# Kept outputs in PSUM beside the scores, block queries and keys by group, a quarter of one streamed pair on chip

## The chip, the core and the metric

The kernel runs on one core of a Trainium2 chip. The core has four compute engines: TensorE (PE in the profile, its weight loads PEld), VectorE (DVE), ScalarE (ACT) and GpSimd (POOL). SyncE (SP) issues most of the transfers, ScalarE and GpSimd issue a few; all of them share 16 DMA engines. SBUF is the working memory on chip. PSUM is the memory into which TensorE writes: 8 banks of 2 KB in each of the 128 partitions, all of them taken in the part of the kernel that is changed. The metric is device time in microseconds (us) of one execution. The kernel before takes 2104.58 us in the median of 3 runs (2098.04 to 2108.45).

## What is computed

There are two independent halves on 2048 tokens. The first is a convolution layer (a short shift filter, then a long convolution by Fourier transforms); the change doesn't touch it. The second is attention with a recurrent memory:

```python
for s in range(n_seg):                       # 64 segments of 32 tokens
    h = concatenate([mem, x_s])              # 8 memory rows and 32 tokens: 40 rows
    q, k, v = h @ Wq, h @ Wk, h @ Wv         # 32 heads of 128, model width 1024
    scores = where(mask, q @ k.T * scale, -1e9)
    o = (softmax(scores) @ v) @ Wo
    mem = o[:8]                              # the memory of the next segment
    outs.append(o[8:])
```

The next segment's memory is the output of this one, so the 64 segments follow each other. The weights are 32 MB in bfloat16, more than SBUF holds.

## The kernel before, in words

Up to about 390 us the kernel computes the first half, and beside it all queries, keys and values of the last 8 tokens of every segment, which need no memory: 512 rows at once ("block" rows). Block queries and keys go to DRAM as `QKBd`, block values as `VBd`. In the loop over segments only 8 memory rows and 24 tokens are left, 32 columns of `hT`.

A "pair" is a 128x2048 piece of weights: 1024 columns each of Wq and Wk (`("qk", group, chunk)`), of two value blocks (`("v", half, chunk)`), or of two heads of Wo (`("o", group, pair)`). Most pairs stay in SBUF. Those in `STREAM`, 17 in each segment, are loaded again in every segment into a ring of 5 places (`wring`); two are parked in PSUM and copied into the ring (L750, L751). `place` (L679) issues the load of the next streamed pair on SP's queue. `done` calls it as soon as TensorE has used a streamed pair, so a load waits for the place that this release frees, and the ring never holds more than five pairs.

The order of the work in a segment is written out by hand, and each engine runs its instructions in that order. The 32 heads are four groups of 8, u0 to u3. For each group: `qk_part` (L784) multiplies by the 8 chunks, `qk_out` (L790, ScalarE) casts the result to `qks`, `tr_a` transposes it by four matmuls into the tile `tp` (L811) and copies it out (L820, L821 on ScalarE; L819 on POOL adds the block keys from `qkb`), `scores` makes the scores `S` (L841 to L852) and takes off their maximum on VectorE (L855, L856), `softmax` runs on ScalarE and VectorE (L864 to L873), `blocks` copies the probabilities into place (L883), and `pv` (L890) multiplies by the values of the segment and the block values `VB`. `pv` has two results in one PSUM tile: ScalarE copies the outputs of the 32 rows (L894, `OT`), VectorE copies the "kept" outputs of the 8 block rows to `OL` (L896). When all groups are done POOL stores `OL` to DRAM (L898, `OLd`); after the loop all kept outputs are multiplied by Wo together. `wo` (L905) multiplies `OT` by Wo, `Y_sb` is the segment's output (L1013), four stores on POOL write it (L1017), and `fill_mem` (L924, L925) transposes it into `hT`, from which the next segment starts. `h_rows` (L916, L917) has put the next tokens into `hT` before.

The work of different groups is interleaved. Around the change the order is: `pv(u0)`, `blocks(u1)`, two chunks of u3, `tr_a(u2)`, four chunks of u3, `scores(u2)`, `softmax(u2)`, and one group later the same with `pv(u1)`, `tr_a(u3)`, `scores(u3)`. On VectorE the copy of kept outputs in `pv(u0)` stands behind the whole of `softmax(u1)`.

In PSUM four banks park weights, three hold accumulators (`ps_a`), and one (`ps_ts`) serves in turn the transposes `tp`, the scores `S`, the transposed tokens and the transposed memory. `OL` is a bfloat16 tile in SBUF. `load_b` (L825) loads the block queries and keys of all four groups of the next segment in one transfer on SP's queue, behind the scores of u3. `load_vb` (L835) loads `VB` on POOL's queue at the end of a segment, behind the stores of `Y_sb`.

Of the kernel before, what the change touches and what calls it, by code (L numbers as in the profile page):

```python
# [9 lines left out]
BF = mybir.dt.bfloat16  # L10
# [11 lines left out]
def fused_kernel(ctx: ExitStack, tc, q, k, v, shift_k, ssm_k, ssm_D, outa, x, mem0, Wq, Wk, Wv, Wo, outb, n_seg):  # L22
# [18 lines left out]
    PARKED = {("qk", 0, 4): ("v", 0, 2), ("v", 0, 3): ("qk", 1, 6)}  # L41

# [631 lines left out]
    def place():  # L674

        if todo:
            key = todo.pop(0)
            t = ring.tile([128, 2, 1024], BF, tag="wring", name="wring")
            nc.sync.dma_start(t[:], Wst[key])  # L679
            placed.setdefault(key, []).append(t[:])  # L680
# [64 lines left out]
    ps_ts = pp.enter_context(tc.tile_pool(name="b_ps_ts", bufs=1, space=PSUM))  # L745

# [19 lines left out]
    VB = act.tile([128, 256], BF, name="VB")  # L766
# [3 lines left out]
    OL = act.tile([128, 32, 8], BF, name="OL")  # L770
# [37 lines left out]
    def transposes(src):  # L808
        tp = ps_ts.tile([128, 512], BF, tag="ts", name="tp")
        for j in range(4):  # L810
            nc.tensor.transpose(tp[:, j * 128:(j + 1) * 128], src[:, j * 128:(j + 1) * 128], ident[:])  # L811
        return tp

    def tr_a(u):
        tp = transposes(u.qks)
        tv = tp[:].rearrange("e (j t c r) -> e t c j r", j=4, t=2, c=2)
        QK = acte.tile([128, 8, 72], BF, tag="qks", name="QK")
        u.QT, u.KT = QK[:, :, 0:32], QK[:, :, 32:72]
        nc.gpsimd.tensor_copy(u.KT[:, :, 32:40], u.qkb.rearrange("e (h t r) -> e t h r", h=8, t=2)[:, 1])  # L819
        nc.scalar.copy(u.QT.rearrange("e (c j) r -> e c j r", c=2), tv[:, 0])  # L820
        nc.scalar.copy(u.KT[:, :, 0:32].rearrange("e (c j) r -> e c j r", c=2), tv[:, 1])  # L821

    def load_b(s):
        qkb = acte.tile([128, 4, 128], BF, tag="qkb", name="qkb")
        nc.sync.dma_start(qkb[:], QKBd[:, :, s * 128:(s + 1) * 128].rearrange("g e x -> e g x"))  # L825
        return qkb

    def new_u(g):
        u = G()
        u.g = g  # L830
        u.qkb = qkb[:, g, :]
        return u

    def load_vb(s):
        nc.gpsimd.dma_start(VB[:], VBd[:, :, s].rearrange("c g r x -> (c g) r x"))  # L835

    def scores(u):
        S = ps_ts.tile([128, 4, 40], F32, tag="ts", name="S")
        qb = u.qkb.rearrange("e (h t r) -> e h t r", h=8, t=2)
# [45 lines left out]
    def pv(u, s):  # L885
        ot = ps_a.tile([128, 512], F32, tag="a", name="otacc")
        for i in range(2):
            o = ot[:, 160 * i:160 * i + 160]
            for kb, w in enumerate((u.v[:, u.g % 2, :], VB[:])):
                nc.tensor.matmul(o, lhsT=w[:, i * 128:(i + 1) * 128], rhs=PB[:, 2 * kb + i].rearrange("p c q -> p (c q)"),  # L890
                                 start=(kb == 0), stop=(kb == 1))
# [4 lines left out]
        nc.vector.tensor_copy(to[:, 8 * u.g:8 * u.g + 8, :].rearrange("e (c i) r -> e i c r", i=2), ov[:, :, :, 32:40])  # L896
# [15 lines left out]
    def h_rows(H_, hT_, r0):  # L912

        tp = ps_ts.tile([128, 1024], BF, tag="ts", name="x_tp")
# [6 lines left out]
    def fill_mem(hT_, Ysrc):  # L921
        tp = ps_ts.tile([128, 512], BF, tag="ts", name="mt_tp")
# [9 lines left out]
    load_vb(0)  # L932
    qkb = load_b(0)
# [3 lines left out]
    for s in range(n_seg):  # L937
# [11 lines left out]
        qk_part(u0, range(5, 8))  # L949
        qk_out(u0)  # L950
        v_part(0, range(0, 4))
        tr_a(u0)
        unpark()
# [5 lines left out]
        qk_part(u1, range(4, 8))  # L959
        qk_out(u1)  # L960
# [15 lines left out]
        qk_part(u2, range(4, 8))  # L976
        qk_out(u2)
        pv(u0, s)
# [7 lines left out]
        qk_part(u3, range(6, 8))  # L986
        qk_out(u3)
        v_part(1, range(0, 1))
        pv(u1, s)
# [5 lines left out]
        if not last:  # L995
            H = load_h(s + 1)
            qkb = load_b(s + 1)
        softmax(u3, S)
        v_part(1, range(5, 8))
        u2.v = u3.v = v_out()  # L1000
        Y = ps_a.tile([128, 512], F32, tag="a", name="yacc")
        wo(u0, Y)
        pv(u2, s)
# [3 lines left out]
        pv(u3, s)  # L1007
        if not last:
            hT = new_hT()
            h_rows(H, hT, 8)  # L1010
        wo(u3, Y)
# [6 lines left out]
        if not last:  # L1018
            load_vb(s + 1)

# [87 lines left out]
```

## Time and profile before

| what | value |
|---|---|
| three runs | 2098.04, 2104.58, 2108.45 us |
| profiled execution: its time, its span | 2100.65, 2098.9 us |
| the loop over segments | from about 395 to 2022 us |
| after it: the kept outputs by Wo | to 2095 us |
| busy in the span: PE, DVE, ACT, POOL | 81%, 53%, 43%, 20% |
| granted TensorE clock, mean | 0.981 |
| moved by DMA | 728.64 MB, mean 347 GB/s |
| DMA share and rate from 400 to 2010 us | 0.99, 366 GB/s |

The page's second part cuts the span into 40 slices; a digit is the busy share of a slice in tenths. Its sixth part lists the DMA issues with size and time from issue to landing. The chain of waits follows the work that ended last back to what released it; a DMA in it lasts from issue to landing. The timeline lists instructions with their start, their duration, their tile and, in brackets, how long the engine was idle before and what ended that. Matmul ends in it are modelled.

### The profile page before, as it was taken

The page shows a single profiled execution, that of the slowest core. Times are in us where ns is not written, and L with a number is a line of the kernel's source. Part 1 is how long each engine was busy: PE and PEld are TensorE (multiplying, and loading weights), DVE is VectorE, ACT ScalarE, POOL GpSimd, SP SyncE. Part 2 cuts the span into 40 slices and gives each one's busy share as a digit, 9 for nine tenths or more (in the row PEclk, how much of TensorE's full clock was granted, in tenths as well). Part 3 has the DMA queues.
Part 4 walks back from the last instruction along what each step waited for, and adds up shares of the span by engine and source line. Part 5 has one row for each costly group of instructions (what it writes and reads, how often), then busy time and mean ns, then how long its engine had stood idle before and what let it go on. Part 6 is the DMA issues. An engine that isn't in the chain of part 4 may idle for free. (4 is left out here: it accounts for less than half of the span.)

```text
span 2098.9 us, 73980 instructions
## 1 busy us (share of the span) xinstructions
PE 1707.5 (81%) x30484; PEld 893.0 (43%) x30514; DVE 1122.1 (53%) x3368; ACT 910.0 (43%) x2278; POOL 417.6 (20%) x1023
## 2 busy tenths in 40 slices
PE   5888987777878888888888888888888878888779
PEld 3332233344444444444444444444444444444449
DVE  8985833355555555555555555555555555555441
ACT  5556741244444444444444444444444444444430
POOL 3003730111111221111111111111112211111110
PEclk9999999999999999999999999999999999999999
DMA  7799989899999999999999999999999999999980
GB/s 272 260 338 331 351 300 378 313 365 361 367 353 367 373 370 367 366 362 370 379 363 368 359 378 365 365 374 363 374 355 369 366 362 365 369 377 370 344 335 22
DMA packets 266384, 728.64 MB, mean 347 GB/s; under 512 B 65007, under 2 KB 77183, under 8 KB 265277
## 3 DMA queue, kind: packets, MB, share of 16 engines
q1 hardware_dynamic: 239534, 686.72, 88.7%
q0 software_dynamic: 15520, 22.06, 3.3%
q10 hardware_dynamic: 10992, 15.14, 2.1%
q8 instruction: 239, 3.92, 0.7%
q14 instruction: 99, 0.81, 0.1%
HBM read 673.52 MB, written 56.56 MB: 348 GB/s over the span
## 5 line engine op out<-in xcount | busy, mean ns | idle before, releaser
L784 PE MATMUL qkacc<-Wqk,hT 128*32 128x512 bf16 x4096 | 335.5, 380 | 0.0
L784 PEld LDWEIGHTS <-hT 128*32 128x32 bf16 x8192 | 185.8, 96 | 238.0 <-issue 82.3
L905 PEld LDWEIGHTS <-OT 128*32 128x32 bf16 x8192 | 210.3, 96 | 109.3 <-issue 61.3
L784 PE MATMUL qkacc<-wring,hT 128*32 128x512 bf16 x2048 | 205.7, 390 | 24.7 <-DMA wring<-Wstqk 17.8
L751 DVE COPY wring<-park 128x1024 bf16<-128x1024 bf16 x128 | 88.5, 692 | 244.0 <-PE vacc L798 112.9
L864 ACT ACTIVATE P<-S 128x128 bf16<-128x128 f32 x256 | 71.1, 278 | 329.1 <-DVE S L856 257.9
L798 PE MATMUL vacc<-Wv,hT 128*32 128x512 bf16 x2560 | 209.3, 381 | 0.0
L798 PE MATMUL vacc<-wring,hT 128*32 128x512 bf16 x1536 | 154.6, 389 | 62.1 <-DMA wring<-in_B_Wv_dram 60.3
L750 ACT COPY wring<-park 128x1024 bf16<-128x1024 bf16 x128 | 130.7, 1021 | 150.9 <-PE qkacc L784 132.7
L798 PEld LDWEIGHTS <-hT 128*32 128x32 bf16 x4096 | 112.5, 96 | 181.7 <-issue 105.7
L784 PE MATMUL qkacc<-Wearly,hT 128*32 128x512 bf16 x2048 | 165.6, 401 | 24.4 <-DVE hT L925 17.9
L883 DVE COPY PB<-P 32x160 bf16<-32x160 bf16 x896 | 173.1, 193 | 10.6
L868 DVE TENSOR_REDUCE sm<-P 128x4 f32<-128x256 bf16 x256 | 107.5, 420 | 131.0 <-ACT P L865 131.0
L820 ACT COPY QK<-tp 128x256 bf16<-128x256 bf16 x256 | 95.4, 373 | 181.7 <-PE tp L811 181.7
L819 POOL COPY QK<-qkb 128x64 bf16<-128x64 bf16 x256 | 60.8, 237 | 566.3 <-PE tp L811 398.2
L905 PE MATMUL yacc<-wring,OT 128*32 128x256 bf16 x2520 | 126.5, 274 | 38.1 <-DMA wring<-Wsto 36.6
L894 ACT CAST OT<-otacc 128x256 bf16<-128x256 f32 x256 | 98.9, 386 | 127.6 <-PE otacc L890 127.6
L790 ACT CAST qks<-qkacc 128x512 bf16<-128x512 f32 x256 | 151.1, 590 | 2.2 <-PE qkacc L784 1.6
L811 PE MATMUL tp<-ident,qks 128*128 128x128 bf16 x1024 | 101.9, 222 | 57.2 <-ACT qks L790 52.7
L1017 POOL DMA_DIRECT2D out_dram<-Y_sb x256 | 128.6, 509 | 92.1 <-ACT Y_sb L1013 89.8
L890 PE MATMUL otacc<-PB,vsb 128*128 128x160 bf16 x512 | 97.8, 238 | 35.9 <-ACT vsb L805 35.9
L855 DVE TENSOR_REDUCE mx<-S 128x4 f32<-128x160 f32 x256 | 83.1, 325 | 74.5 <-PE S L852 68.4
(219 smaller groups left out, 2973.8 us busy)
## 6 DMA issues: line engine op xcount, KB each, us to landing
wring<-Wstqk SPq DMA_DIRECT2D x448, 512.0 KB, 6.1
wring<-in_B_Wv_dram SPq DMA_DIRECT2D x320, 512.0 KB, 6.6
wring<-Wsto SPq DMA_DIRECT2D x315, 512.0 KB, 6.3
SK<-s_sb SPq DMA_DIRECT2D x8, 1024.0 KB, 5.7
SU<-s_sb SPq DMA_DIRECT2D x8, 1024.0 KB, 6.7
QKBd<-stq ACTq DMA_DIRECT2D x4, 2048.0 KB, 8.2
Kg<-SK SPq DMA_DIRECT2D x16, 512.0 KB, 7.7
Ug<-SU SPq DMA_DIRECT2D x16, 512.0 KB, 8.0
```

Source lines behind the costliest of these rows:

```text
L750: nc.scalar.copy(t[:, 0, :], park[key][0][:])
L784: nc.tensor.matmul(u.qk[p0:p0 + 32, :], lhsT=hT[:, kc, :], rhs=w[:, t, c2 * 512:(c2 + 1) * 512], start=(kc == 0), stop=(kc == 7), tile_pos ...
L790: nc.scalar.copy(u.qks[:], u.qk[:])
L798: nc.tensor.matmul(vacc[0][32 * c:32 * c + 32, :].rearrange("p (n x) -> p n x", n=2), lhsT=hT[:, kc, :], rhs=w[:, :, c * 256:(c + 1) * 256 ...
L811: nc.tensor.transpose(tp[:, j * 128:(j + 1) * 128], src[:, j * 128:(j + 1) * 128], ident[:])
L820: nc.scalar.copy(u.QT.rearrange("e (c j) r -> e c j r", c=2), tv[:, 0])
L868: nc.vector.tensor_reduce(out=sm[:], in_=Pv.rearrange("p b x k -> p x b k"), op=ALU.add, axis=AX.XY)
L883: (nc.vector if by[c] == "D" else nc.gpsimd).tensor_copy(to, src)
L890: nc.tensor.matmul(o, lhsT=w[:, i * 128:(i + 1) * 128], rhs=PB[:, 2 * kb + i].rearrange("p c q -> p (c q)"), start=(kb == 0), stop=(kb == 1))
L894: nc.scalar.copy(u.OT[:].rearrange("e (c i) q -> e i c q", i=2), ov[:, :, :, 0:32])
L905: nc.tensor.matmul(Y[32 * dq:32 * dq + 32, 0:256], lhsT=u.OT[:, hh, 0:32], rhs=w[:, hh % 2, dq * 256:(dq + 1) * 256], start=(u.g == 0 and ...
L1017: nc.gpsimd.dma_start(outb[32 * s:32 * s + 24, dq * 256:(dq + 1) * 256], Y_sb[32 * dq + 8:32 * dq + 32, :])
```

## The change

There are four edits, all in the loop over segments.

1. Of the streamed pair `("qk", 1, 3)` the last 512 of 2048 columns stay on chip in a tile `Wquarter`, loaded once. In every segment `place` loads the other 1536 columns into the ring, and the matmul of these columns reads `Wquarter`.
2. The bank `ps_ts` holds one tile, `TS`. Its first 512 bfloat16 columns serve the transposes and the scores as before. Its other half, as 256 float32 columns, is `OL`: VectorE copies the kept outputs of each group from one PSUM tile to the other. At the end of a segment (`store_kept`) VectorE copies all of `OL` to a bfloat16 tile `OLst` in SBUF, and POOL stores that one. For the last group the copy stands behind `h_rows`.
3. `VB` and `OLst` share one buffer, and `load_vb` is issued after `tr_a(u0)` of the segment that uses it, not at the end of the segment before.
4. Block queries and keys are loaded group by group, 32 KB each, into two buffers in turn. The loads of groups 2 and 3 are issued behind the chunks of u1 and u2 in the same segment, those of groups 0 and 1 of the next segment behind the chunks of u3 and of the second half of the values.

```diff
+    QUARTER = ("qk", 1, 3)
...
-            nc.sync.dma_start(t[:], Wst[key])
+            if key == QUARTER:
+                nc.sync.dma_start(t[:].rearrange("p n d -> p (n d)")[:, 0:1536],
+                                  Wst[key].rearrange("p n d -> p (n d)")[:, 0:1536])
+            else:
+                nc.sync.dma_start(t[:], Wst[key])
...
+    TS = ps_ts.tile([128, 1024], BF, name="ts")
+    OL = TS[:, 512:1024].bitcast(F32).rearrange("e (h r) -> e h r", h=32)
+    Wquarter = act.tile([128, 512], BF, name="Wquarter")
+    nc.sync.dma_start(Wquarter[:], half_src(QUARTER, 1)[:, 512:1024])
...
-    VB = act.tile([128, 256], BF, name="VB")
-    OL = act.tile([128, 32, 8], BF, name="OL")
...
-                    nc.tensor.matmul(u.qk[p0:p0 + 32, :], lhsT=hT[:, kc, :], rhs=w[:, t, c2 * 512:(c2 + 1) * 512],
+                    own = ("qk", u.g, kc) == QUARTER and t == 1 and c2 == 1
+                    nc.tensor.matmul(u.qk[p0:p0 + 32, :], lhsT=hT[:, kc, :],
+                                     rhs=Wquarter[:] if own else w[:, t, c2 * 512:(c2 + 1) * 512],
...
     def transposes(src):
-        tp = ps_ts.tile([128, 512], BF, tag="ts", name="tp")
+        tp = TS[:, 0:512]
...
+    def load_b(s, g):
+        qkbs.append(acte.tile([128, 128], BF, tag="qkb", name="qkb", bufs=2))
+        nc.sync.dma_start(qkbs[-1][:], QKBd[g, :, s * 128:(s + 1) * 128])
...
     def load_vb(s):
+        VB = act.tile([128, 256], BF, tag="VB", name="VB")
         nc.gpsimd.dma_start(VB[:], VBd[:, :, s].rearrange("c g r x -> (c g) r x"))
+        return VB
...
-        S = ps_ts.tile([128, 4, 40], F32, tag="ts", name="S")
+        S = TS[:, 0:320].bitcast(F32).rearrange("p (a k) -> p a k", a=4)
...
-        to = OL[:] if s + 1 < n_seg else OLs[:, s]
-        nc.vector.tensor_copy(to[:, 8 * u.g:8 * u.g + 8, :].rearrange("e (c i) r -> e i c r", i=2), ov[:, :, :, 32:40])
-        if u.g == 3 and s + 1 < n_seg:
-            nc.gpsimd.dma_start(OLd[:, s], OL[:].rearrange("e h r -> e (h r)"))
+        to = OL if s + 1 < n_seg else OLs[:, s]
+
+        def keep():
+            nc.vector.tensor_copy(to[:, 8 * u.g:8 * u.g + 8, :].rearrange("e (c i) r -> e i c r", i=2), ov[:, :, :, 32:40])
+
+        if u.g < 3:
+            keep()
+        return keep
+
+    def store_kept(s):
+        OLst = act.tile([128, 256], BF, tag="VB", name="OLst")
+        nc.vector.tensor_copy(OLst[:], OL.rearrange("e h r -> e (h r)"))
+        nc.gpsimd.dma_start(OLd[:, s], OLst[:])
...
         tr_a(u0)
+        VB = load_vb(s)
...
         qk_part(u1, range(4, 8))
+        u1.qkb = qkbs.pop(0)
+        load_b(s, 2)
         qk_out(u1)
...
-        pv(u3, s)
+        keep = pv(u3, s, VB)
         if not last:
             hT = new_hT()
             h_rows(H, hT, 8)
+        keep()
+        if not last:
+            store_kept(s)
         wo(u3, Y)
...
-        if not last:
-            load_vb(s + 1)
```

More of the change, by code (lines that the diff above doesn't have):

```diff
@@ L818, in tr_a @@
         u.QT, u.KT = QK[:, :, 0:32], QK[:, :, 32:72]
-        nc.gpsimd.tensor_copy(u.KT[:, :, 32:40], u.qkb.rearrange("e (h t r) -> e t h r", h=8, t=2)[:, 1])
+        nc.gpsimd.tensor_copy(u.KT[:, :, 32:40], u.qkb[:].rearrange("e (h t r) -> e t h r", h=8, t=2)[:, 1])
         nc.scalar.copy(u.QT.rearrange("e (c j) r -> e c j r", c=2), tv[:, 0])
         nc.scalar.copy(u.KT[:, :, 0:32].rearrange("e (c j) r -> e c j r", c=2), tv[:, 1])
[L823 to L826, printed above, removed]
+    qkbs = []
+    def load_b(s, g):
+        qkbs.append(acte.tile([128, 128], BF, tag="qkb", name="qkb", bufs=2))
+        nc.sync.dma_start(qkbs[-1][:], QKBd[g, :, s * 128:(s + 1) * 128])
     def new_u(g):
@@ L830, in new_u @@
         u.g = g
-        u.qkb = qkb[:, g, :]
         return u
     def load_vb(s):
+        VB = act.tile([128, 256], BF, tag="VB", name="VB")
         nc.gpsimd.dma_start(VB[:], VBd[:, :, s].rearrange("c g r x -> (c g) r x"))
+        return VB
     def scores(u):
-        S = ps_ts.tile([128, 4, 40], F32, tag="ts", name="S")
-        qb = u.qkb.rearrange("e (h t r) -> e h t r", h=8, t=2)
+        S = TS[:, 0:320].bitcast(F32).rearrange("p (a k) -> p a k", a=4)
+        qb = u.qkb[:].rearrange("e (h t r) -> e h t r", h=8, t=2)
         for c in range(4):
@@ L883, in blocks, with pv @@
                 (nc.vector if by[c] == "D" else nc.gpsimd).tensor_copy(to, src)
-    def pv(u, s):
+    def pv(u, s, VB):
         ot = ps_a.tile([128, 512], F32, tag="a", name="otacc")
@@ L912, in h_rows @@
     def h_rows(H_, hT_, r0):
-        tp = ps_ts.tile([128, 1024], BF, tag="ts", name="x_tp")
+        tp = TS[:, 0:512]
         for half in range(2):
@@ L921, in fill_mem @@
     def fill_mem(hT_, Ysrc):
-        tp = ps_ts.tile([128, 512], BF, tag="ts", name="mt_tp")
+        tp = TS[:, 0:512]
         for half in range(2):
@@ L930, in new_hT @@
         return acte.tile([128, 8, 32], BF, tag="hT", name="hT")
-    load_vb(0)
-    qkb = load_b(0)
+    load_b(0, 0)
+    load_b(0, 1)
     home_o(late_o[7], [homes[i][:] for i in (2, 3)])
@@ L949, in fused_kernel @@
         qk_part(u0, range(5, 8))
+        u0.qkb = qkbs.pop(0)
         qk_out(u0)
@@ L976, in fused_kernel @@
         qk_part(u2, range(4, 8))
+        u2.qkb = qkbs.pop(0)
+        load_b(s, 3)
         qk_out(u2)
-        pv(u0, s)
+        pv(u0, s, VB)
         blocks(u1, "DDDD")
@@ L986, in fused_kernel @@
         qk_part(u3, range(6, 8))
+        u3.qkb = qkbs.pop(0)
+        if not last:
+            load_b(s + 1, 0)
         qk_out(u3)
         v_part(1, range(0, 1))
-        pv(u1, s)
+        pv(u1, s, VB)
         blocks(u2, "DDDD")
@@ L996, in fused_kernel @@
             H = load_h(s + 1)
-            qkb = load_b(s + 1)
         softmax(u3, S)
         v_part(1, range(5, 8))
+        if not last:
+            load_b(s + 1, 1)
         u2.v = u3.v = v_out()
@@ L1002, in fused_kernel @@
         wo(u0, Y)
-        pv(u2, s)
+        pv(u2, s, VB)
         blocks(u3, "DDAA")
@@ L1010, in fused_kernel @@
             h_rows(H, hT, 8)
+        keep()
+        if not last:
+            store_kept(s)
         wo(u3, Y)
```

## The prediction

> **What bounds the kernel now.** I read the page first: the slices of the span, then the DMA issues. The memory's loop runs from about 400 to 2020 us, and in it the DMA engines are busy in nine tenths or more of every slice, at 360 to 378 GB/s, while no compute engine reaches nine tenths.
>
> ```profile
> PE   5888987777878888888888888888888878888779
> DMA  7799989899999999999999999999999999999980
> ...
> wring<-Wstqk SPq DMA_DIRECT2D x448, 512.0 KB, 6.1
> wring<-in_B_Wv_dram SPq DMA_DIRECT2D x320, 512.0 KB, 6.6
> wring<-Wsto SPq DMA_DIRECT2D x315, 512.0 KB, 6.3
> ...
> qkb<-QKBd SPq DMA_DIRECT2D x64, 128.0 KB, 5.1
> ...
> VB<-VBd POOLq DMA_DIRECT2D x64, 64.0 KB, 5.1
> ...
> OLd<-OL POOLq DMA_DIRECT2D x63, 64.0 KB, 5.5
> ```
>
> The last column is issue to landing. A streamed pair is 524,288 B; in the first microsecond of a segment, where the moved rate averages 393 GB/s over 29 segments read in windows of 1 us, that is 1.33 us. Landing 6.1 to 6.6 us after issue means that a pair has some four pairs before it. So the stream is nearly always behind, and DMA time is worth something. How much, the chain of waits tells: it alternates between stretches like these two.
>
> ```profile
> 1736.39 6.77 DMA wring<-in_B_Wv_dram
> 1743.20 0.42 PE vacc L798 x4
> 1743.64 6.77 DMA wring<-Wsto
> 1750.45 0.43 PE yacc L905 x8
> ...
> 1789.48 0.43 DVE sm L868
> 1790.14 0.44 DVE P L870
> 1793.18 0.43 DVE sm L868
> 1793.84 0.44 DVE P L870
> 1794.30 0.45 DVE P L873
> 1796.79 0.49 ACT vsb L805
> 1797.32 0.45 PE otacc L890 x4
> ```
>
> The first is a ring place waiting for its load, round after round. The second, from 1789 to 1797, has no DMA in it: softmax of the second, third and fourth group. Two limits thus lie close together. I therefore read the timeline of the 62 segments between 410 and 2010 us at the same rows (hT ready is the end of L925's copy; "max" the start of L855's reduction of a group; groups 0 to 3; pv the matmuls of L890). Stage, mean, tenth percentile in us: hT ready to max of group 1: 10.06, 9.43. Max 1 to max 2: 3.75, 3.70. Max 2 to max 3: 3.71, 3.70. Max 3 to pv 2: 1.71, 1.69. Pv 2 to pv 3: 2.74, 2.24. Pv 3 to the next hT: 3.60, 3.07. Sums: 25.56, the mean period, and 23.83. The middle (max 1 to pv 2) hardly varies: it is a latency chain through VectorE, and the stream costs nothing there. The other three stages hold the 1.7 us lost to late pairs. I call 23.83 the floor and 25.56 the most that the stream can need, since the DMA share of the loop is 0.99.
>
> **The change part by part.** *The quarter.* In each segment the load of that pair shrinks from 4 KB to 3 KB in each partition. Bounds: nothing, if a shorter packet takes as long; 0.36 us, by the loop's mean of 366 GB/s. I take 0.33 us (a quarter of 1.33), as pairs move at the rate of bytes. The stream's need falls to 25.23. The one resident load costs 0.33 us once.
>
> *Kept outputs beside the scores.* Here the middle chain matters. The rows of one group in it:
>
> ```profile
> 1201.60 0.33 DVE L855 TENSOR_REDUCE mx<-S 128x4 f32<-128x160 f32 x1
> ...
> 1203.35 0.40 PE L811 MATMUL tp<-ident,qks 128*128 128x128 bf16 x4 [0.26 <-ACT qks L790]
> ...
> 1204.11 0.38 ACT L821 COPY QK<-tp 128x256 bf16<-128x256 bf16 x1
> ...
> 1204.35 0.18 DVE L896 CAST OL<-otacc 128x64 bf16<-128x64 f32 x1
> ...
> 1204.68 0.21 PE L852 MATMUL S<-QK,qkb 128*8 128x40 bf16 x8
> ```
>
> The transposes of group 2 (1203.35) start as soon as ScalarE has cast its queries; the kept outputs of group 0 are copied (1204.35) a microsecond later, at the end of softmax 1. Neither waits for the other: one writes a PSUM bank, the other SBUF. In the changed kernel both write the tile TS. I looked at the waits in the built program: the first transposing matmul of group 2 now waits for VectorE's copy of group 0's kept outputs, and that of group 3 for group 1's copy. Both have nothing to do with each other's data. Over 62 segments that copy ends 1.15 us (group 2) and 1.17 us (group 3) after the transposes now start. The new path is a ring: max 1 to the copy's end 2.94 (means of both groups), to the transposes 0.05 (as from L790's cast), to the end of the scores 1.56, to the next max 0.09, so 4.64 in place of 3.75 and 3.71. The middle grows by 0.89 + 0.93 = 1.8 us per segment. The bounds, by the spread of the rows (0.67 to 1.19 of lateness): 1.2 and 1.9. The scores of group 2 now have 0.4 us before VectorE is free for them (mean 13.45 against 13.81), which is in the sum. Queued behind the waiting matmul on TensorE are the rest of group 3's queries and keys, its streamed pairs' releases, the scores and everything after.
>
> The Trainium skill, page "PSUM — Partial Sum Buffer", section "PSUM bank collisions raise a hardware error", tells kernel authors to guard PSUM by bank and 32-partition quadrant and not by address, since a second engine in the same bank collides even at other columns. By the addresses (columns 0 to 511 and 512 to 1023) the change would add no wait and the sum would be 25.23 per segment, 2080 us; by this rule the waits are needed, and the sum is the one below. The built program is on the rule's side; no run here shows a collision.
>
> *Two more VectorE steps.* The copy of the last group moves behind the copy into hT, and a new 128x256 copy out of PSUM follows. ScalarE's cast of the same 128x256 from PSUM takes 0.39 us; bounds 0.33 (a 128x160 on VectorE) and 0.69 (the 128x1024 parking copy). In the timeline VectorE has 1.7 us idle before L925, which the transposes of Y_sb end. They now also wait for this copy, which would end 0.7 us or more ahead of them. Nothing.
>
> *OL's store and VB.* The store issues some 0.4 us later and lands after 5.5 us, about 4 us into the segment. VB's load is now behind group 0's key copy on POOL (mean 5.0 us) and waits for that landing, because both use one buffer: issue about 5.3, landing 5.1 later, 10.4. Its first reader, pv 0, runs at 10.7 on the mean, so late loads will stall some segments. But pv 0's result is needed only by VectorE's copy at max 1 + 2.8; a stall of up to about 1 us ends inside the new wait of TensorE. Behind VB's load on POOL stands the clearing of P, which waits for Y_sb's stores anyway (4 us or more after their issue). Taken as nothing; at most 0.3 us a segment.
>
> *Block queries and keys by group.* Four loads of 32 KB replace one of 128 KB, with the same 512 packets of 256 B. Around the present load the rate falls to 332, 334 and 349 from 393 GB/s, 0.42 us in all. Bounds: a little below nothing (the packets spread out), and +1.3 if each of four costs as much as the one. I take nothing: cost by packets. SP issues three more at 0.37 us, ahead of pair loads; a pair that lands 6.3 us after issue doesn't notice 0.4. Each load waits for the scores two groups back, which SP's queue has passed by then, and is needed some 6 us later against 5.1 of landing.
>
> *Sum.* The floor becomes 23.83 + 1.8 = 25.63, the need of the stream 25.23. The floor is now the greater. What stays of the 1.7 us lost to late pairs? In the longer middle the stream, four pairs behind, goes on, so it gains up to 1.8 us and 0.33 more; against that the ring has five places and cannot run ahead by more. Bounds of the rest: 0 and 1.4 (nothing gained but the quarter). I take 0.35, nearer to nothing because of the depth of the queue. Period 25.98, +0.42; by 63 segments +26 us. The profiled execution took 2100.65 us around its span of 2098.9; 2100.65 + 26 = 2127. The median of the three runs shown is 4 us above that execution, within their spread (2098 to 2108), so I keep 2127.
>
> **The rivals.** *A: the stream stays the limit and hides the wait.* For it: a DMA share of 0.99, landings of 6.3 us. Then 25.23 a segment, -21 us, 2080. The point that decides is whether the wait adds less than 1.4 us (25.23 - 23.83). Against: both rows give 0.9, and the lowest values of all six stages still add up to 23.6, which with 1.8 is above 25.23. Chance 0.06.
>
> *B: all that was lost to late pairs is paid back.* The floor alone, 25.63: +4 us, 2105. For it: the queue's depth. Against: DMA would still be wanted 98% of the time, and the tenth percentile of all stages at once is seldom met. With a little rest it reaches 2115. Chance 0.20.
>
> *C: the forecast,* a rest of 0.15 to 0.85: 2115 to 2158, likeliest 2127. Chance 0.56.
>
> *D: the ring has run as far ahead as it can before the new waits,* so that they are added nearly whole: 25.56 + 1.8 - 0.33 = 27.03, +93, 2194. For it: TensorE's waits for pairs stand just outside the middle, five places are 6.7 us of stream, and SP's queue waits for releases (334.7 us in all for those of the queries and keys). Against: pairs there too land only 6 us after issue. From 2158 to 2194, chance 0.18.
>
> The quarter does what it says: the built program loads 1536 of 2048 columns and one matmul in four reads the resident tile.
>
> **How the numbers follow.** No change means within 0.5%, 10.5 us, about what a measurement of this kernel tells. A is faster: 0.06. B ends at the bound of 2115: 0.20. C and D lie above it: 0.74. The range leaves out A and D's upper half, 0.15 together: 2096 to 2172.
>
> **What would show it.** Max 1 to max 2 and max 2 to max 3 at 4.6 us in place of 3.7; TensorE's transposes idle on VectorE's copy into ts, near 1.2 us and more, 126 times; fewer waits of vacc and yacc for wring; a DMA share below 0.99; pv 0 waiting for VB now and then. Wrong would be: the middle at 3.7 (the wait isn't there), or the middle at 4.6 and the period at 25.2 (A), or pairs landing after 7 us or more because of the small loads.

## The result, and the profile after

The changed kernel takes 2228.1 us in the median (2215.76 to 2231.78), the kernel before 2107.27 us (2098.04 to 2110.39) beside it. The ratio is 1.056, 95% interval [1.053, 1.059]: slower by some 118 us. The forecast was 2127, with a range of 2096 to 2172. The side was right, the size far off.

The profiled execution after took 2215.76 us, the least of its six, around a span of 2213.9. First its page: two rows of the slices, then DMA issues (size, median us from issue to landing).

```profile
PE   5798977777777777777777777777777777777759
...
DMA  7789999999999999999999999999999999999960
...
wring<-Wstqk SPq DMA_DIRECT2D x384, 512.0 KB, 5.6
wring<-in_B_Wv_dram SPq DMA_DIRECT2D x320, 512.0 KB, 6.5
wring<-Wsto SPq DMA_DIRECT2D x315, 512.0 KB, 5.5
wring<-Wstqk SPq DMA_DIRECT2D x64, 384.0 KB, 6.7
```

The DMA row still shows nines in nearly all of the loop, and TensorE's row has fallen from sevens and eights to sevens. But pairs of Wo now land 5.5 us after issue instead of 6.3, which fits fewer transfers ahead of them. The next to last slice of the DMA row reads 6 where it read 8. The granted clock is a little lower, 0.965 against 0.981, but TensorE's busy time is the same, 1708.3 and 1707.5 us, so the clock doesn't account for the loss.

Now the step that the prediction spoke of, from the timeline after (start, us, engine and line, tiles, idle time before and what ended it). It goes from one group's reduction of the scores' maximum to the next.

```profile
1201.22 0.33 DVE L867 TENSOR_REDUCE mx<-ts 128x4 f32<-128x160 f32 x1
...
1202.76 0.59 ACT L800 CAST qks<-qkacc 128x512 bf16<-128x512 f32 x1 [0.40 <-PE qkacc L793]
...
1204.02 0.23 DVE L910 COPY ts<-otacc 128x64 f32<-128x64 f32 x1
...
1204.31 0.38 PE L821 MATMUL ts<-ident,qks 128*128 128x128 bf16 x4
...
1205.98 0.33 DVE L867 TENSOR_REDUCE mx<-ts 128x4 f32<-128x160 f32 x1 [1.01 <-ACT QK L831]
...
1208.66 0.20 DVE L910 COPY ts<-otacc 128x64 f32<-128x64 f32 x1
...
1208.91 0.38 PE L821 MATMUL ts<-ident,qks 128*128 128x128 bf16 x4 [1.71 <-DVE ts L910]
...
1210.52 0.33 DVE L867 TENSOR_REDUCE mx<-ts 128x4 f32<-128x160 f32 x1 [0.94 <-ACT QK L831]
```

ScalarE has cast the queries at 1203.35, but the transposes (L821) start at 1204.31, right behind VectorE's copy of kept outputs (L910), which ends at 1204.25. The two steps take 4.76 and 4.54 us, where before it was 3.7. The table of waits after (engine, tile and line; what it waited for; us in total, times, longest) has the same:

```profile
PE ts L821 <- DVE ts L910: 174.4, 124, 2.1
...
POOL QK L829 <- DMA qkb<-QKBd: 123.7, 27, 19.5
```

The second row is new too, and its longest wait is 19.5 us. That one stands in the last segment. The chain of waits after ends with these lines; columns are start, us and what it was.

```profile
2107.78 5.77 DMA wring<-in_B_Wv_dram
2113.55 2.64 issue
2120.42 7.41 DMA wring<-in_B_Wv_dram
2127.91 16.68 DMA qkb<-QKBd
2148.99 2.05 PE yacc L926 x51
2153.46 55.69 PE pl L1062 x928
```

A load of 32 KB is on the path for 16.68 us. The timeline of SP's queue and POOL shows why:

```profile
2121.61 0.43 SPq L996 DMA_DIRECT2D Wv<-Wsto  x1
2122.08 2.97 SPq L996 DMA_DIRECT2D Wqk<-Wsto  x4
...
2125.22 0.94 SPq L999 DMA_DIRECT2D Wearly<-OLd  x2
...
2127.91 0.32 SPq L837 DMA_DIRECT2D qkb<-QKBd  x1
...
2144.74 0.24 POOL L829 COPY QK<-qkb 128x64 bf16<-128x64 bf16 x1 [19.50 <-DMA qkb<-QKBd]
```

In the last segment the loads for the final product (five pairs of Wo, then 4 MB of kept outputs, L996 and L999) are issued ahead of the block keys of group 3, which the segment itself still needs.

Where the time went, by the same stages as in the prediction. Means over the 62 segments, us; "last" is from the last hT to the first weight load of the final product.

| | hT to max 1 | max 1 to 2 | max 2 to 3 | max 3 to pv 2 | pv 2 to 3 | pv 3 to hT | period | last |
|---|---|---|---|---|---|---|---|---|
| before | 10.06 | 3.75 | 3.71 | 1.71 | 2.74 | 3.60 | 25.56 | 22.5 |
| after | 10.42 | 4.69 | 4.68 | 1.89 | 2.28 | 3.21 | 27.17 | 41.4 |

62 times 1.61 is 99.8 us, the last segment adds 18.9, and the parts before the loop and after it together give back some 4: 115, the difference of the two spans. What gives back is mainly a wait of 4.1 us of the final product's first matmul for the kept outputs (`PE pl L1031 <- DMA Wearly<-OLd`), which the kernel before has and the changed kernel, later by then, has not; so the hole costs some 15 us on balance. The middle adds 1.91 per segment, as forecast. What was to be paid back elsewhere is 0.30 on balance instead of 1.4. And the last segment was not in the sum at all.

### The profile page after: what moved, and what is told of

Read it like the earlier page. It is cut to its first block, busy times and chain, and to the rows that moved or that the text cites. A ratio compares the mean times of both kernels' runs of the same rounds, so it can differ in the third digit from the quotient of the medians.

```text
span 2213.9 us, 74498 instructions
## 1 busy us (share of the span) xinstructions
PE 1708.3 (77%) x30484; PEld 908.9 (41%) x30514; DVE 1155.8 (52%) x3431; ACT 915.9 (41%) x2278; POOL 411.3 (19%) x1023
## 4 chain that ended last, share of the span: by engine, by line
DMA 34%; PE 33%; DVE 18%; ACT 7%; issue 5%; SPq 1%; POOL 0%; ACTq 0%; DVEq 0%; POOLq 0%
DMA wring<-in_B_Wv_dram 17%; PE qkacc L793 7%; PE yacc L926 7%; DMA wring<-Wstqk 5%; PE vacc L808 4%; DVE P L885 3%; DVE P L882 3%; DVE sm L880 3%; DMA qkb<-QKBd 3%; PE ts L821 3%; PE pl L1062 3%; PE otacc L902 2%; DMA out_dram<-Y_sb 2%; DVE mx L867 2%; DVE ts L868 2%
## 5 line engine op out<-in xcount | busy, mean ns | idle before, releaser
L793 PEld LDWEIGHTS <-hT 128*32 128x32 bf16 x8192 | 179.3, 96 | 235.9 <-issue 82.0
L821 PE MATMUL ts<-ident,qks 128*128 128x128 bf16 x1024 | 100.9, 221 | 183.7 <-DVE ts L910 174.4
L926 PEld LDWEIGHTS <-OT 128*32 128x32 bf16 x8192 | 218.6, 100 | 56.1 <-ACT OT L906 17.4
L830 ACT COPY QK<-ts 128x256 bf16<-128x256 bf16 x256 | 95.4, 373 | 331.3 <-PE ts L821 214.0
L808 PE MATMUL vacc<-Wv,hT 128*32 128x512 bf16 x2560 | 222.9, 406 | 0.0
L808 PE MATMUL vacc<-wring,hT 128*32 128x512 bf16 x1536 | 157.5, 396 | 76.4 <-DMA wring<-in_B_Wv_dram 75.7
L876 ACT ACTIVATE P<-ts 128x128 bf16<-128x128 f32 x256 | 71.1, 278 | 320.2 <-DVE ts L868 275.7
L867 DVE TENSOR_REDUCE mx<-ts 128x4 f32<-128x160 f32 x256 | 83.2, 325 | 226.7 <-ACT QK L831 114.6
L808 PEld LDWEIGHTS <-hT 128*32 128x32 bf16 x4096 | 104.9, 97 | 207.1 <-issue 86.7
L821 PEld LDWEIGHTS <-qks 128*128 128x128 bf16 x1024 | 67.9, 97 | 266.9 <-issue 146.0
L793 PE MATMUL qkacc<-Wearly,hT 128*32 128x512 bf16 x2048 | 160.0, 389 | 21.8 <-DVE hT L946 17.9
```

Of the source, the lines that this page charges most:

```text
L808: nc.tensor.matmul(vacc[0][32 * c:32 * c + 32, :].rearrange("p (n x) -> p n x", n=2), lhsT=hT[:, kc, :], rhs=w[:, :, c * 256:(c + 1) * 256 ...
L867: nc.vector.tensor_reduce(out=mx[:], in_=S[:], op=ALU.max, axis=AX.X)
L926: nc.tensor.matmul(Y[32 * dq:32 * dq + 32, 0:256], lhsT=u.OT[:, hh, 0:32], rhs=w[:, hh % 2, dq * 256:(dq + 1) * 256], start=(u.g == 0 and ...
```

## The experiments

Unless another kernel is named, every ratio is to the kernel before, run beside it; the interval is 95%. Periods and stages are read as above from one profiled execution of each kernel. Executions of one kernel differ by up to 25 us, that is 0.4 us per segment, so a difference of 0.1 or 0.2 between two periods shows nothing by itself.

**The quarter alone.** The kernel before, with three quarters of the pair loaded.

```diff
+            if key == ("qk", 1, 3):
+                nc.sync.dma_start(t[...][:, 0:1536], Wst[key][...][:, 0:1536])
+            else:
                 nc.sync.dma_start(t[:], Wst[key])
```

> The kernel before with the quarter alone: the pair (qk, 1, 3) is loaded in 1536 of 2048 columns, and the matmul of the other 512 columns reads 512 columns of another resident pair, so part of the second group's keys is computed from other weights; everything else is as before. If the stream's time is what the loop waits for, a quarter pair of 1.33 us gives 0.33 us in each of 64 segments, 21 us less than before (2086), and not less than 10 us. If a shorter packet takes as long, or the latency chain of softmax is the limit, no change.

Measured: 2099.9 us, ratio 0.996 [0.994, 0.998], -8 us or 0.13 per segment. The bytes at the loop's rate would be 0.33.

**Half of that pair not loaded.**

> The kernel before with half of the pair (qk, 1, 3) not loaded in any segment; the matmuls of that half read another resident chunk, so that part of the computation is changed. The same with a quarter gave -8 us, 0.13 us per segment, where a quarter of a pair at the rate of bytes would be 0.33 to 0.36. Theory 'lateness comes from the ring's depth, so that fewer bytes give less than their time': half a pair gives -12 to -25 us (0.2 to 0.4 per segment). Rival 'bytes count in full, and the quarter's run was off': -40 to -46 us (0.65 to 0.72 per segment).

Measured: 2096.3 us, ratio 0.997 [0.994, 0.999], -7 us: no more than for the quarter, and less than the theory's 12 too. Bytes that are taken out here are worth a fraction of their time, and not in proportion.

**The bank alone.** The kernel before with edit 2, `OLst` in a buffer of its own; loads as before.

```diff
+    TS = ps_ts.tile([128, 1024], BF, name="ts")
+    OL = TS[:, 512:1024].bitcast(F32).rearrange("e (h r) -> e h r", h=32)
...
-        tp = ps_ts.tile([128, 512], BF, tag="ts", name="tp")
+        tp = TS[:, 0:512]
```

> The kernel before with the second edit alone: kept outputs as float32 in the bank of the scores, copied to SBUF and stored at the end of a segment. Block queries and keys, VB and the pairs are loaded as before. Theory W (the two new waits of the transposes lengthen the chain by 1.8 us a segment, and the stream pays almost nothing back): the middle stages at 4.6 us, the period at 27.0 us or more, 85 to 110 us more than before (2190 to 2215). Rival G (the waits are mostly hidden, and the small loads of queries and keys cost the rest): the middle at 4.6, but a period of 25.7 to 26.2 us, 10 to 40 us more than before.

Measured: 2212.4 us, ratio 1.048 [1.044, 1.052]; period 27.32, the middle at 4.60 and 4.60, last segment 23.4. In its table of waits:

```profile
PE ts L812 <- DVE ts L899: 193.3, 126, 1.7
...
PE vacc L799 <- DMA wring<-in_B_Wv_dram: 66.7, 109, 2.2
...
PE qkacc L785 <- DMA wring<-Wstqk: 37.2, 62, 1.6
...
PE yacc L915 <- DMA wring<-Wsto: 12.1, 23, 1.3
```

and in that of the kernel before:

```profile
PE vacc L798 <- DMA wring<-in_B_Wv_dram: 60.3, 116, 2.1
...
PE yacc L905 <- DMA wring<-Wsto: 36.6, 76, 1.3
...
PE qkacc L784 <- DMA wring<-Wstqk: 17.8, 34, 1.2
```

The wait on VectorE stands there without any other edit, 126 times. The wait of the Wo products for late pairs has fallen to 12.1 us (36.6 before), but that of the value products has grown from 60.3 to 66.7 and that of the queries and keys from 17.8 to 37.2. In all TensorE waits 116.0 us for pairs, where it waited 114.7: the waits have moved, and none of them is saved. This one edit costs 101 to 105 us.

**The loads by group alone.** The kernel before with edit 4.

```diff
+        u1.qkb = qkbs.pop(0)
+        load_b(s, 2)
         qk_out(u1)
...
-            qkb = load_b(s + 1)
```

> The kernel before with the fourth edit alone: block queries and keys loaded group by group into two buffers. In the last segment the load of the last group stands behind 6.5 MB of final loads on SP's queue, which should cost about 15 us once, as in the changed kernel. Theory W: the period of the other segments stays at 25.5 to 25.7 us, in all 10 to 25 us more than before. Rival G: the period rises by 0.7 us or more, and in all 60 to 100 us more than before.

Measured: 2163.2 us, ratio 1.026 [1.022, 1.030]; period 26.51, last segment 40.6. The edit costed at nothing costs 54 to 56 us. The profiled execution, whose stages these are, took 2173.34 us, some 10 more than the other three: it is 73 us above that of the kernel before, 0.95 in each of 62 segments and some 15 in the last one. In the median execution the part per segment is nearer to 0.7. This lies between theory W and rival G. Its timeline, in two groups of one segment:

```profile
1203.84 0.42 SPq L827 DMA_DIRECT2D qkb<-QKBd  x1
...
1207.14 0.49 SPq L827 DMA_DIRECT2D qkb<-QKBd  x1
...
1210.56 0.24 POOL L819 COPY QK<-qkb 128x64 bf16<-128x64 bf16 x1 [3.40 <-DMA qkb<-QKBd]
...
1210.85 0.23 PE L847 MATMUL S<-QK 128*32 128x40 bf16 x8 [0.78 <-POOL QK L819]
```

POOL waits for block keys, and TensorE's scores wait for POOL: 41 segments of 62 in group 2, 61 of 62 in group 3. The landing takes 5.7 us in the median, which the prediction had; but the loads of groups 2 and 3 go out at 7.96 and 11.55 us of the segment, and POOL wants them at 12.4 and 16.1, by the times of its key copies in the kernel before. That leaves 4.5 us.

**The last segment mended, in the changed kernel.** Group 3's load goes ahead of the final loads in the last segment only.

```diff
         if last:
+            load_b(s, 3)
             spare = ...
...
-        load_b(s, 3)
+        if not last:
+            load_b(s, 3)
```

> The changed kernel with one load moved: in the last segment the block queries and keys of the last group are loaded ahead of the final loads, not behind them. If the hole of 17 us in the last segment comes from that order alone, 14 to 16 us less than the changed kernel (about 2213). If the final loads hold up that segment anyway (something else waits for them), less than 5 us.

Measured: 2207.6 us, ratio 1.046 [1.042, 1.049], 20 us under the changed kernel; last segment 24.8 in place of 41.4, period 27.25 (27.17 unmended). The hole is what it looked like. Some 3 of the 16.6 come back at once, as the final product again waits for its kept outputs; 14 to 16 us were expected, and the larger difference of the two medians lies within what executions differ by.

**The waits taken away, in the changed kernel.** VectorE copies the kept outputs of groups 0 and 1 right behind the sum of the softmax, ahead of its other three steps; ScalarE copies `OT` after that.

```diff
         nc.vector.tensor_reduce(out=sm[:], ...)
+        return P, Pv, sm
+
+    def softmax2(u, P, Pv, sm):
         nc.vector.reciprocal(sm[:], sm[:])
...
         pv(u0, s, VB)
+        softmax2(u1, *sums)
```

> The changed kernel with one step of VectorE's order moved: the kept outputs of groups 0 and 1 are copied right behind the sum of the next group's softmax (1.7 us after its maximum), no longer behind its transpose (2.9 us after); ScalarE's copy of the 32 rows follows it. The copies still go to the bank of the scores. Theory W (the wait of the transposes is what the bank costs): the copy ends about when the transposes are ready, max 1 to max 2 falls from 4.66 to 3.75 or a little more where a group's load is late, the period from 27.2 to the 26.5 us of the groups alone, and the time to about 2165 to 2180 with the hole of the last segment in it. If sharing the bank itself slows the engines (the copies or matmuls take longer), no gain or a small one.

Measured: 2177.9 us, ratio 1.036 [1.033, 1.040]; period 26.60. In the table of waits of this version:

```profile
POOL QK L829 <- DMA qkb<-QKBd: 386.8, 101, 20.0
...
PE ts L821 <- DVE ts L911: 39.7, 80, 0.8
```

TensorE's wait falls from 174.4 to 39.7 us, and the next thing that is late shows itself: the block keys, 386.8 us of POOL's waiting, as in the version with the loads alone. In the changed kernel the longer waits had hidden part of this.

**The waits taken away, and the loads issued earlier.** The same, with each load right behind the scores that free its buffer.

```diff
         S = scores(u0)
+        load_b(s, 2)
...
         S = scores(u3)
         if not last:
             H = load_h(s + 1)
+            load_b(s + 1, 1)
```

> The same, and the loads of block queries and keys are issued right behind the scores that free their buffer, about 1.3 us earlier, in the last segment also ahead of the final loads. Theory L (the loads by group cost because they land late for POOL's copy of the block keys): max 1 to max 2 and max 2 to max 3 at 3.7 to 3.8, period 25.4 to 25.8, time 2090 to 2115, about that of before. Rival D (four small loads take more of the DMA engines' time than one): the DMA busy time stays near 26 us a segment, period 26.0 us or more, time 2130 or more.

Measured: 2106.1 us, ratio 1.001 [0.997, 1.004]; period 25.51, the middle at 3.85 and 3.75, last segment 23.4. This is called the level version below. Two changes of order take out all of the 118 us. All four edits are still in it; memory is saved, and the time is that of the kernel before.

**One load later again.** The stage from pv 2 to pv 3 had grown to 3.17 in that version.

> The changed kernel with the early copy of kept outputs and the loads behind the scores (2106 us, 25.51 us per segment), except that the load of group 1 for the next segment stands again behind the chunks of the second half of the values, as in the change. In the version before this one the stage from pv 2 to pv 3 had grown to 3.19 us from 2.39. Theory 'that load stands ahead of pairs that Wo waits for': the stage back to 2.4 to 2.8, period 25.1 to 25.3, total 2080 to 2092. Rival 'the stream as a whole is late, and the wait only shows there': the time reappears in another stage, period 25.4 to 25.8, total 2098 to 2125.

Measured: 2108.1 us, ratio 1.002 [0.999, 1.005]; the stage stays at 3.10. The load was not the cause; pairs are late, and the wait shows in one stage or another.

**A ring of seven.** The kernel before with two more places. Two resident pairs read their neighbours' weights to make room, so the three kernels with seven places leave out part of the computation: they measure the stream and are no solution.

```diff
-    RING = 5
+    RING = 7
+    ALIAS = {("v", 0, 7): ("v", 0, 6), ("qk", 2, 1): ("qk", 2, 0)}
```

> The kernel before with a ring of 7 places in place of 5. Room is made by letting two resident pairs, (v, 0, 7) and (qk, 2, 1), use the weights of their neighbours (v, 0, 6) and (qk, 2, 0), so these parts of the values and of group 2's queries and keys are computed from other weights, and four loads of 256 KB before the loop are left out. As control for the next run. If late pairs come from the ring's depth, the period falls below 25.2 us (2080 or less); if the DMA engines are simply busy all the time, it stays within 0.2 us of 25.56.

Measured: 2030.7 us, ratio 0.966 [0.962, 0.971]; period 24.42. The loop alone in the kernel before, as one window (us, busy time and instructions of PE, PEld, DVE, ACT, POOL, granted clock, DMA share, GB/s):

```profile
424.40:2009.20 1584.80, 1293.75 (x27032) 686.07 (x27032) 830.96 (x2853) 696.75 (x1922) 302.27 (x869) 0.99 0.99 366
```

and with seven places:

```profile
423.80:1938.10 1514.30, 1245.00 (x27032) 669.86 (x27032) 832.41 (x2852) 699.35 (x1922) 303.63 (x869) 0.99 1.01 383
```

The same 17 pairs per segment move in 24.42 us instead of 25.56, at 383 GB/s instead of 366. TensorE's waits for value pairs, in the table of waits with seven places, are gone:

```profile
PE vacc L802 <- DMA wring<-in_B_Wv_dram: 1.1, 2, 0.7
...
PE yacc L909 <- DMA wring<-Wsto: 0.3, 1, 0.3
```

**The bank with a ring of seven.**

> The kernel before with the shared bank alone (as in the run of that edit) and a ring of 7 places, made as in the control. Theory R (the stream could pay back the new waits but for its five places): with seven the period falls from 27.3 to 25.7 to 26.4 us, 1.0 us or more of the 1.76 comes back, and the rates at the end of a segment no longer fall to 260 GB/s. Rival: the waits stand in the chain from segment to segment whatever the stream does, and hT ready to max 1 still takes 10 us; then the period stays above 26.8.

Measured: 2157.0 us, ratio 1.026 [1.022, 1.029]; period 26.51, the middle at 4.62 and 4.61, waits for pairs 0.08 us per segment. With no pair late the waits cost 26.51 - 24.42 = 2.09 per segment. With five places late pairs cost 25.56 - 24.42 = 1.14 before, and 27.32 - 26.51 = 0.81 beside the bank. So the longer middle paid back 0.33. The medians say the same: the bank adds 105 us with five places and 126 with seven, 21 us or 0.34 per segment apart. The result lies between the two expectations: 0.81 came back with the two places, but the 2.09 stays in the chain from segment to segment whatever the stream does. Of it 1.80 is in the two middle stages and 0.30 in the next one (2.00 to pv 2 against 1.70).

**The bank with early copies,** loads as before. This tells the two waits from all else that the bank brings.

> The kernel before with the kept outputs in the scores' bank (edit 2) and VectorE's copies of groups 0 and 1 right behind the sums of the softmax, ScalarE's copies of OT after them; the loads are those of the kernel before. Edit 2 with the copies in their old place gave 2212 us (27.32 us per segment). Theory 'the bank costs only by its two waits': the middle back to 3.6 to 3.9 per step, period 25.4 to 25.7, total 2095 to 2115. Rival 'the early order is itself faster and pays for the loads by group in the version that came out level with before': period 24.8 to 25.1, total 2060 to 2075. Rival 'the bank costs in other places too': period 26 or more, total 2130 or more.

Measured: 2105.0 us, ratio 1.000 [0.997, 1.003]; period 25.67, the middle at 3.66 and 3.65. So the bank costs by its two waits; all else that it brings, the new copy into `OLst` and the copy behind `h_rows` among it, is within 0.3% of nothing.

**Early copies alone,** kept outputs in SBUF.

> The kernel before, kept outputs in SBUF, with the early order of VectorE's and ScalarE's copies alone. Nothing waits for the kept outputs here, so by the theory of the waits it should be level: period 25.4 to 25.7, total 2095 to 2115. Rival 'the early order is itself faster, by getting the steps behind the softmax out of order': period 24.8 to 25.2, total 2060 to 2085.

Measured: 2103.8 us, ratio 0.999 [0.996, 1.003]. The order itself gives nothing.

**Loads by group, issued earlier, alone.** The kernel before with edit 4, the loads issued where the level version issues them.

> The kernel before with the loads of block queries and keys by group alone (edit 4), but each load issued right behind the scores that free its buffer: groups 2 and 3 behind the scores of u0 and u1, groups 0 and 1 of the next segment behind those of u2 and u3. With the loads placed as in the change this cost +56 us (26.51 us per segment against 25.56, and a hole of about 18 us in the last segment). Theory 'the loads cost because they land late, behind the pairs that are ahead of them': period 25.5 to 25.7, last segment 22 to 25 us, total 2100 to 2120. Rival 'four small loads cost DMA time, whenever they are issued': period 26.2 to 26.5, total 2145 to 2160.

Measured: 2140.0 us, ratio 1.017 [1.013, 1.022]; period 26.15, last segment 23.0. Between the two expectations. The middle is back at 3.72 and 3.76 and the last segment is mended, yet 0.59 per segment stays. It sits in the stage to max 1 (10.74), where TensorE waits for value pairs 0.65 us longer per segment than before.

**The same with VB's load at the start of the segment.**

> The kernel before with the loads by group issued behind the scores, as in the run that gave 2140 us (26.15 us per segment), and the load of VB moved from the end of the segment to behind the key transposes of u0, as edit 3 of the change has it. In the run before this one the rate from 24 us of a segment to 2 us of the next had fallen to 291 to 342 GB/s from 376 to 396, and TensorE's waits for value pairs at 2 to 6 us had grown by 0.65 us per segment. Theory 'the load of VB meets the small loads at the end of the segment': period 25.4 to 25.7, total 2095 to 2115. Rival 'the small loads cost by themselves, the place of VB is not it': period 26.0 to 26.4, total 2130 to 2155.

Measured: 2140.7 us, ratio 1.013 [1.008, 1.018]; period 26.29. VB's place is not it. This is also edit 3 without the shared buffer: it costs nothing that can be seen.

**Loads by group with a ring of seven.**

> The kernel before with the loads by group issued behind the scores and a ring of 7 places in place of 5; two resident pairs read the weights of their neighbours to make room, so that part of the computation is changed. With the one load and 7 places the loop took 24.42 us per segment (2031 us). Theory 'the small loads cost only by making pairs late, which seven places hide': period 24.4 to 24.6, total 2028 to 2045. Rival 'the small loads cost transfer time or hold up SyncE's queue': about as much is added as with five places, period 24.9 to 25.1, total 2060 to 2080.

Measured: 2071.5 us, ratio 0.981 [0.977, 0.984]; period 25.10. That is 0.68 above the ring of seven with one load, with no pair late. The rows of the waits that carry it, in this version:

```profile
POOL QK L823 <- DMA qkb<-QKBd: 216.9, 76, 4.4
POOL P L866 <- DMA out_dram<-Y_sb: 206.9, 63, 5.4
...
ACT P L868 <- DMA out_dram<-Y_sb: 132.0, 61, 4.2
```

and, of the same table, with one load and seven places:

```profile
POOL P L866 <- DMA out_dram<-Y_sb: 171.8, 62, 4.5
...
ACT P L868 <- DMA out_dram<-Y_sb: 90.0, 52, 3.9
```

Two things are longer. In the middle (0.32 more) POOL still waits for block keys, in 28 of 62 segments in group 2 and in 46 in group 3. At the start (0.48 more) the clearing of `P` and ScalarE's first write to it wait for the stores of `Y_sb`, which share its buffer, and these land 5.9 us after issue in the table of DMA issues, with one load 5.2. That the small loads themselves slow these stores is not shown: the bank with a ring of seven has one load, and there the stores land after 5.5.

**Which partner makes the loads free?** The loads, issued early, cost 35 us beside the kernel before and nothing that can be seen in the level version, where bank, quarter and early copies are too. First the level version without the quarter:

> The changed kernel with early copies and early loads (2106 us, level with before), but with the whole pair loaded in every segment. Beside the kernel before the quarter gave 8 us. Theory 'the edits add up, and the loads cost nothing beside the bank': 2110 to 2120, period 25.5 to 25.8. Rival 'the quarter is what makes room for the small loads': period 26.1 to 26.4, total 2130 to 2150.

Measured: 2109.4 us, ratio 1.000 [0.996, 1.003]. Then loads, VB's place and early copies, without bank and quarter:

> The kernel before with the loads by group behind the scores, VB's load at the start of the segment and the early order of the copies, kept outputs in SBUF, no quarter. Without the early order this took 2141 us (26.29 us per segment). Theory 'it is the place of the kept outputs or the quarter that goes well with the loads': unchanged, period 26.1 to 26.4, total 2130 to 2150. Rival 'the early order is what the loads go well with': period 25.5 to 25.8, total 2100 to 2120.

Measured: 2136.2 us, ratio 1.012 [1.007, 1.017]. Neither the quarter nor the early order is the partner. What is left between these two is the place of the kept outputs: in PSUM, copied once and stored from `OLst` behind `h_rows`, with one buffer for `OLst` and `VB`. With it the stores of `Y_sb` land after 5.0 us and TensorE waits 58.3 us for value pairs, without it 5.5 and 97.0. The traces show where: from 2 us before a segment's start to 3 us after it, a 4 KB packet of a pair takes 170 ns with it and 191 without, 167 in the kernel before. But in the bank alone, which has no small loads, it takes 182, so they aren't the cause by themselves. Why the packets are slower there, no run shows.

## Why the prediction was wrong, step by step

**Right: the waits.** The transposes of groups 2 and 3 wait for VectorE's copy, 124 times of the 126 forecast, and the middle runs at 4.69 and 4.68 where 4.64 was worked out. The version with early copies shows that the bank costs nothing else that can be seen. The step was decided by the built program's waits, with the rule of the Trainium skill beside them, page "PSUM — Partial Sum Buffer", section "PSUM bank collisions raise a hardware error". The trace shows the wait that the program holds, the copy's end 0.06 us before the transposes' start (1204.25 and 1204.31), though the two write different columns of the bank; what would happen without the wait, no run here shows.

**Wrong, and the largest term: "What stays of the 1.7 us lost to late pairs?", where 0.35 was taken.** Two readings failed in it. The floor was not 23.83. It was made of six tenth percentiles, which don't occur in one segment (the shortest of the kernel before took 24.35); without late pairs the segment takes 24.42. So late pairs cost 1.14, not 1.7. And of these 0.33 came back, not nearly all. In the prediction's terms, 23.83 + 1.8 + 0.35 = 25.98 was forecast, and the bank alone measured 24.42 + 2.09 + 0.81 = 27.32: the floor was 0.59 too low, the new waits 0.29, the rest 0.46. Rival D described the loop (27.03 against 27.17 measured), in part by luck: its 0.33 was the quarter, which gave 0.13, and about as much came back from late pairs instead. Its upper end of 2194 us is still below the measured time, for the last segment was in no rival either. Its ground is in the waits of SP's queue. Before:

```profile
SPq L679 <- PE qkacc L784: 334.7, 378, 9.2
...
SPq L679 <- PE yacc L905: 170.2, 288, 1.6
...
SPq L679 <- PE vacc L798: 84.4, 188, 2.1
```

After:

```profile
SPq L685 <- PE qkacc L793: 402.7, 370, 3.2
SPq L685 <- PE vacc L808: 237.7, 213, 4.4
...
SPq L685 <- PE yacc L926: 95.4, 164, 1.7
...
SPq L682 <- PE yacc L926: 75.9, 63, 1.5
```

The queue that feeds the ring waits longer for TensorE to release places, 812 us by these rows where it was 589 (L682 issues the quarter's pair), while its waits that end with a pair's landing fall from 428 to 263 us. While TensorE waits for VectorE it uses no pair, and the five places are full or on their way. Averaged over 29 segments in windows of 1 us, the DMA share is 0.75 to 0.90 from 20 to 24 us of the segment after, and 0.98 to 1.03 before. The prediction had the five places among its bounds and gave more weight to the landing of 6.3 us. Of what it named as signs, the waits of the Wo products for pairs did vanish, but those of the value products grew from 60.3 to 75.7 us.

**Wrong: "25.56 the most that the stream can need, since the DMA share of the loop is 0.99".** As an upper bound it held, but it was used as the need. The ring of seven moves the same pairs in 24.42. The Trainium skill, page "Perfetto Trace Analysis", section "Identifying the Most-Contended Engine", advises against judging DMA by the time its engines are busy and for judging it by the memory's use. The runs agree: a share of 0.99 at 366 GB/s and of 1.01 at 383 are told apart by the rate alone. Rival A, the stream as the limit, rested on that bound.

**Wrong: "Block queries and keys by group. I take nothing: cost by packets."** 0.95 per segment alone in the profiled execution, inside the bounds of the text (up to 1.3) and at the wrong end. The comparison of "needed some 6 us later against 5.1 of landing" compared a mean with a median and left no margin; the landing is 5.7. That part goes away with the order. A rest of 0.5 to 0.7 beside the kernel before doesn't; it sits at the segment's start, and its cause is open. The Trainium skill, page "DMA: Bandwidth & Descriptors", section "Rules for kernel authors", says to merge small transfers, since under 64 KB one pays mostly overhead. The pair of runs with seven places agrees in direction (four loads of 32 KB cost 0.68 more than one of 128 KB, of which 0.32 is POOL's wait for late loads); the level version, where the same loads cost nothing that can be seen, does not.

**Missed: the last segment.** The text reads 62 segments in the middle of the loop and multiplies by 63. That group 3's load is now issued inside the segment, and in the last one behind 6.5 MB of final loads on the same queue, could be read in the code. It holds the last segment up by 17 to 19 us, and costs 14 to 15 on balance.

**Mis-sized: the quarter,** 0.13 per segment for 0.33. Half a pair gave no more. It fits that pairs were late by the ring's depth, since a shorter load does not open a place; no run tests that apart.

**Right: the copies of `OLst` and of group 3, and VB.** Nothing that can be seen, as taken: the level version has them all. TensorE does wait for VB now and then; here, after (weight loads of pv, and POOL's issue of the load):

```profile
PEld L902 <- DMA VB<-VBd: 13.1, 20, 2.1
...
POOL VB L846 <- DMA OLd<-OLst: 10.6, 10, 2.1
```

The second row is POOL's wait for the store that shares VB's buffer, 10 times in 62.

The single edits don't add up: 105 for the bank, 54 to 56 for the loads, -8 for the quarter make about 150, and together they cost 118. A load that is late by a microsecond costs nothing where the transposes wait a microsecond for VectorE anyway: POOL waits 379.1 us for block keys with the loads alone, and 123.7 in the changed kernel.

What stays open is why the loads by group are free beside kept outputs in PSUM, and why packets of the pairs and small stores are slower around a segment's start in some versions. No complete version beat the kernel before. The one lever that moved it, two more places in the ring, needs 8 KB per partition; the change frees memory too, but spends it on the quarter.

## What to carry to other kernels

A stream with a DMA share of 0.99 can still be limited by its number of places: look at what the issuing queue waits for, and if it waits for releases, as here, a longer chain on the compute side can be added nearly whole and fewer bytes give little. A "floor" for a stage chain has to come from segments that occurred, not from a sum of each stage's best. When a load moves from one iteration to another, walk through the last iteration by itself, and compare its landing with the earliest time it can be needed once the other waits are gone.

## What the runs showed of the hardware

Four loads of 32 KB in place of one of 128 KB, with the same 512 packets of 256 B of data, cost 0.68 us per segment with no pair late. Stores land later beside them (12 KB: 5.9 us against 5.2), but the bank with one load, also with seven places, has 5.5. The page counts 3,072 packets under 512 B more, before 65,007, after the loads alone 68,079: 16 for each of the 192 added issues, so every issue brings 16 small packets of its own; in the traces they are of 4 bytes.

The same DMA share of 0.99 to 1.01 stood for 366 GB/s with five loads in the ring and 383 with seven, and a pair's landing went from 6.1-6.6 to 7.0-7.3 us at the same time: with more in flight the stream was faster and each transfer slower.
